# Weights converted in the first batch's first stage, stores issued by ACT, most of batch 1's first stage moved into the main loop, and the transform put ahead of the inner product

## The chip, the cores and the metric

The kernel runs on one core of a Trainium2 chip. A core has TensorE (PE, with its weight loads shown apart as PEld), VectorE (DVE), ScalarE (ACT), GpSimd (POOL), SyncE (SP, which here only issues transfers) and 16 DMA engines. The metric is the device time of one execution in microseconds; the runs before have a median of 1624.6 us (1624.46 to 1625.23, three runs).

## The reference

For 8 batches of 3136 rows by 256 columns the input is filtered in the frequency domain along the rows and then goes through a gated feed-forward layer:

```python
X = np.fft.rfft(x, axis=1)
y = np.fft.irfft(X * (filt_r + 1j * filt_i)[None], n=3136, axis=1)
h = np.maximum(y @ w_in, 0.0)                  # 256 -> 1024
conv = sum(conv_w[k] * shifted(h, k - 1) for k in range(3))   # along the rows, zero padded
out = (h / (1.0 + np.exp(-conv))) @ w_out      # 1024 -> 256
```

The weights w_in, conv_w and w_out arrive as float64.

## The kernel before, in words

**Transform.** The 3136-point transform is done by matrix products in four stages of 14 tiles each (a tile is a pair of the 28 columns of a 112 x 28 arrangement of the rows, 512 columns wide). Stage 1 multiplies rows of x by tables (line 231, `by_column`), ACT copies the bank (`store`, line 226) and a transfer (227) stores it in the DRAM buffer `a_dram` of the batch. Stage 2 (`second`, 235 and 238) reads `a_dram` back; the filter follows as three DVE passes (`filt`, 244 to 246) and a POOL addition (247). Stage 3 is `by_column` again, its result is stored in `b_dram`. Stage 4 (`fourth`, 255) reads `b_dram` and makes y. Stages 2 and 4 need all 14 tiles of the stage before them. All values are split in a high and a low part, so that three fp32r products stand for one fp32 product: y's high part is an ACT pass (145), its low part a subtraction on DVE (148) or POOL (151).

**Ahead of the main loop.** Batch 0 goes through its four stages here. In the code before, the 16 weight pieces (8 times one of w_in and one of w_out) are turned from float64 to f32 by seven DVE instructions and one POOL addition a pair (`to_f32`, 159 to 173) and split by ACT (145) and POOL (151). These steps are handed out as a generator, four at a time, among the tiles of the second and third stage, and six at a time among those of the fourth. Also among the tiles of the fourth stage stands the whole first stage of batch 1. Row tiles have 6, 5 and 4 buffers by stage, a PSUM pool has 5 banks. SP issues every transfer, in an order that a scheduler sets; PE, DVE, ACT and POOL keep the order of the code (`manual_schedule`).

**Main loop.** The 8 batches are cut in 56 units of 448 rows, and a step m is one of the 8 feature blocks of a unit: 448 steps, 56 a batch. In a step PE does `inner` (176 to 178, y times w_in, six matmuls into one of four banks), and `project` of the step six earlier (471 to 473, nine or twelve matmuls). Between, ACT does `relu` (427), `centre` (431), `sigmoid` (438) and the rounding of g (145); DVE two more taps (435) and the gate (441); POOL the low part of g (151). When a unit's projection is complete, DVE copies it out (`evacuate`, 486). The transform of batch t, its stages 2 to 4, and stage 1 of batch t+1 ride in the 56 steps of batch t-1: a table `plan` says which transform tiles a step holds. `transform(op)` does a tile's matmuls into one of two banks (`ps_t`), `from_bank(op)` empties the bank a step later: ACT copies it for stages 1 and 3, DVE filters it for stage 2 and copies it for stage 4. Inputs are loaded five tiles ahead (`tin`), and a stage's loads wait until the stage before is stored in full. Engines work in order, so an instruction that waits holds up all that stand behind it on its engine.

Of the kernel before, what the change touches and what calls it, by code (L numbers as in the profile page):

```python
# [124 lines left out]
def tile_fft_filter_gated_ffn(  # L125
# [98 lines left out]
    def store(pool, kind, b, q, ps, bufs, tag):  # L224
        st = pool.tile([112, 2, D], F32, name=tag, bufs=bufs)
        nc.scalar.activation(st, ps[0:112].rearrange("p (j d) -> p j d", d=D), AF.Copy)
        nc.sync.dma_start(out={"1": a_out, "3": b_out}[kind][b][:, pair(q)], in_=st)
# [32 lines left out]

    with (
        tc.tile_pool(name="sp", bufs=2) as sp,
        tc.tile_pool(name="sps", bufs=5, space=bass.MemoryType.PSUM) as sps,
        tc.manual_schedule(engines=COMPUTE),
# [3 lines left out]
        def load_weights(k):  # L268
            raws[k] = raw = sp.tile([128, 2, 512], I32, name="raw")
            for part, src in enumerate((w_in, w_out)):  # L270
                nc.sync.dma_start(out=raw[:, part], in_=src[:, 512 * k:512 * k + 512])

        def convert_conv():
            n = 3 * NF
            raw = sp.tile([128, 2, 512], I32, name="raw")
            nc.sync.dma_start(out=raw[:, 0, 0:2 * n], in_=conv_w)
            yield
            em = sp.tile([128, 2, 512], I32, name="em", bufs=1)
            yield from to_f32(cw.rearrange("p k f -> p (k f)"), raw[:, 0, 0:2 * n], em[:, 0, 0:n], em[:, 1, 0:n])

        def convert_weights():

            for k in range(8):
                raw = raws.pop(k)
                em = sp.tile([128, 2, 512], I32, name="em", bufs=1)
                ws = sp.tile([128, 2, 256], F32, name="ws", bufs=1)
                yield from to_f32(ws.rearrange("p t n -> p (t n)"), raw.rearrange("p t n -> p (t n)"), em[:, 0], em[:, 1])
                yield
                parts = [[t.rearrange("p a b -> p (a b)")[:, 256 * k:256 * k + 256] for t in w] for w in (wi, wo)]
                for part, (wh, wl) in enumerate(parts):  # L290
                    hi_act(wh, ws[:, part])
                yield
                for part, (wh, wl) in enumerate(parts):
                    lo_pool(wl, ws[:, part], wh)
                    yield
                if k < 6:
                    load_weights(k + 2)

        def table(kind, c):
            k, src = {"1": (112, s1), "3": (120, i1)}[kind]  # L300
            tabs[kind, c] = t = sp.tile([120, 4, 112], F32, name=f"tab{kind}", bufs=3)[0:k]
            nc.sync.dma_start(out=t, in_=src[:, 4 * c:4 * c + 4])
# [6 lines left out]
        def copy_filter(q):  # L309
# [3 lines left out]
            if q == NP - 1:  # L313
                nc.sync.dma_start(out=f[92:93, 1, 0], in_=nyq)

        def psum():
            return sps.tile([128, 512], F32, name="ps")

        csteps, wsteps = convert_conv(), convert_weights()

        def x_load(q):
            rows["1", q] = load_in(sp, "1", 0, q, 6, "x")

        def a_load(q):
            rows["2", q] = load_in(sp, "2", 0, q, 5, "a")

        for c in range(3):
            table("1", c)
            x_load(2 * c)
            x_load(2 * c + 1)  # L330
        nc.sync.dma_start(out=s2_sb, in_=s2[:, 0:120])
        nc.sync.dma_start(out=s2s_sb, in_=s2s[:, 0:120])
        nc.sync.dma_start(out=m2_sb, in_=m2)
        for q in range(NP):
            ps = psum()
            by_column(ps, tabs["1", q // 2][:, 2 * (q % 2):2 * (q % 2) + 2], rows.pop(("1", q)))
            store(sp, "1", 0, q, ps, 3, "sa")
            if q % 2 and q // 2 + 3 < 7:
                table("1", q // 2 + 3)
# [324 lines left out]
```

## Time and profile before

| what | value |
|---|---|
| median of the runs | 1624.6 us |
| profiled execution, its own time | 1620.7 us |
| its span, first to last instruction | 1618.9 us |
| PE busy, share of the span | 1527.6 us, 94% |
| DVE, ACT, POOL busy | 1203.6, 1202.6, 878.3 us |
| bytes moved, mean rate | 238.7 MB, 147 GB/s |
| first inner product of the main loop | 152 us |

The profile is one execution. Its windows give busy time of each engine in a stretch of the span, its groups give instructions by line with their mean duration, and its waits give who waited for whom; a releaser in it is inferred. Busy PE time counts overlapping matmuls once, so the time of a step is read from the starts of its first matmuls. The mean over the whole span hides that the first 152 us are worked by other engines than the rest.

### The profile page before, as it was taken

The numbers are of one execution on the slowest core, as the hardware profiler recorded it, in microseconds if no ns is written. First come the engines' busy times: TensorE is split into PE (matmuls) and PEld (weight loads), VectorE is DVE, ScalarE is ACT, GpSimd is POOL, SyncE is SP. The second block draws the span as 40 slices with busy tenths as digits, with TensorE's granted clock in tenths as the row PEclk, the third lists the DMA queues.
The fourth block names the chain that finished last, engine by engine and source line by source line (L and its number), as shares of the span: only waits on it lengthen the run. The fifth ranks groups of instructions, "written<-read, shape, count | busy, mean of one in ns | idle before, by whom it ended". The sixth has DMA issues, their size and how long they took to land.

```text
span 1618.9 us, 28466 instructions
## 1 busy us (share of the span) xinstructions
PE 1527.6 (94%) x9424; PEld 1363.0 (84%) x9424; DVE 1203.6 (74%) x1966; ACT 1202.6 (74%) x2623; POOL 878.3 (54%) x1170
## 2 busy tenths in 40 slices
PE   4658999999999999999999999999999999999999
PEld 2237788998899887998899988899889988899998
DVE  0875887768876788667877688767887788777776
ACT  3326667986688766987678866788668866799987
POOL 0541454755566555664557555575556745576554
PEclk8758999999999999999999999999999999999999
DMA  9768655355554555446553565545554435320001
GB/s 284 209 205 252 185 167 168 108 166 171 161 164 129 168 157 176 132 133 174 183 177 106 143 190 167 160 115 172 168 163 147 125 119 174 97 75 24 23 24 37
DMA packets 171491, 238.73 MB, mean 147 GB/s; under 512 B 16696, under 2 KB 119121, under 8 KB 171345
## 3 DMA queue, kind: packets, MB, share of 16 engines
q1 hardware_dynamic: 171345, 236.92, 49.3%
q8 instruction: 75, 1.23, 0.3%
q14 instruction: 71, 0.58, 0.1%
HBM read 159.78 MB, written 77.07 MB: 146 GB/s over the span
## 4 chain that ended last, share of the span: by engine, by line
PE 73%; issue 9%; DVE 6%; POOL 6%; DMA 3%; ACT 2%; SPq 1%; POOLq 0%; DVEq 0%; ACTq 0%
PE po L471 10%; PE po L472 9%; PE po L473 9%; PE ps_h L177 9%; PE ps_h L178 9%; PE ps_h L176 9%; PE ps_t L231 8%; PE ps_t L255 5%; POOL g L151 4%; PE ps_t L235 2%; DVE t L435 2%; POOL gm L151 1%; DMA a_dram<-sa 1%; DVE v L246 1%; DVE v L245 1%
## 5 line engine op out<-in xcount | busy, mean ns | idle before, releaser
L435 DVE SCALAR_TENSOR_TENSOR t<-ps_h,cw,t 128x448 f32<-128x448 f32 x896 | 609.2, 680 | 283.0 <-ACT t L431 278.3
L151 POOL TENSOR_TENSOR g<-t,g 128x384 fp32r<-128x384 f32 x448 | 455.1, 1016 | 182.5 <-ACT g L145 72.8
L431 ACT ACTIVATE t<-ps_h,cw 128x448 f32<-128x448 f32 x448 | 284.9, 636 | 231.1 <-POOL gm L151 206.2
L471 PE MATMUL po<-wo,g 128*128 128x256 f32 x1344 | 413.5, 308 | 1.9 <-DVE ot L486 1.9
L473 PE MATMUL po<-wo,g 128*128 128x256 f32 x1344 | 374.4, 279 | 0.0
L472 PE MATMUL po<-wo,g 128*128 128x256 f32 x1344 | 374.2, 278 | 0.0
L247 POOL TENSOR_TENSOR z<-z,v 120x512 f32<-120x512 f32 x112 | 147.6, 1318 | 390.0 <-DVE v L246 341.3
L176 PE MATMUL ps_h<-y,wi 128*128 128x450 f32 x896 | 330.8, 369 | 1.2 <-ACT y L145 1.2
L177 PE MATMUL ps_h<-y,wi 128*128 128x450 f32 x896 | 330.2, 369 | 0.6 <-DVE y L148 0.6
L178 PE MATMUL ps_h<-y,wi 128*128 128x450 f32 x896 | 328.3, 366 | 0.0
L441 DVE TENSOR_TENSOR t<-ps_h,t 128x448 f32<-128x448 f32 x448 | 275.7, 616 | 0.6 <-ACT t L438 0.6
L427 ACT ACTIVATE ps_h<-ps_h 128x450 f32<-128x450 f32 x448 | 250.9, 560 | 32.6 <-PE ps_h L178 30.8
L471 PEld LDWEIGHTS po<-wo,g 128*128 128x128 f32 x1344 | 253.6, 189 | 21.2 <-issue 9.9
L472 PEld LDWEIGHTS po<-wo,g 128*128 128x128 f32 x1344 | 253.5, 189 | 13.4 <-issue 10.3
L438 ACT ACTIVATE t<-t 128x448 f32<-128x448 f32 x448 | 255.9, 571 | 0.9 <-DVE t L435 0.8
L473 PEld LDWEIGHTS po<-wo,g 128*128 128x128 f32 x1344 | 253.7, 189 | 0.0
L145 ACT ACTIVATE g<-t 128x384 fp32r<-128x384 f32 x448 | 231.9, 518 | 10.4 <-PE po L472 9.7
L151 POOL TENSOR_TENSOR y<-z,y 128x448 fp32r<-128x448 f32 x98 | 139.2, 1421 | 124.0 <-ACT y L145 110.1
L178 PEld LDWEIGHTS ps_h<-y,wi 128*128 128x128 f32 x896 | 168.8, 188 | 14.2
L176 PEld LDWEIGHTS ps_h<-y,wi 128*128 128x128 f32 x896 | 169.6, 189 | 9.4 <-issue 1.6
L177 PEld LDWEIGHTS ps_h<-y,wi 128*128 128x128 f32 x896 | 169.1, 189 | 7.8 <-issue 1.1
L151 POOL TENSOR_TENSOR gm<-t,gm 128x64 fp32r<-128x64 f32 x448 | 145.9, 326 | 0.0
(73 smaller groups left out, 1992.9 us busy)
## 6 DMA issues: line engine op xcount, KB each, us to landing
filt<-in_filt SPq DMA_DIRECT2D x98, 512.0 KB, 4.2
tin<-a_dram SPq DMA_DIRECT2D x98, 224.0 KB, 3.4
b_dram<-st SPq DMA_DIRECT2D x98, 224.0 KB, 4.2
tin<-b_dram SPq DMA_DIRECT2D x98, 224.0 KB, 2.7
out<-ot SPq DMA_DIRECT2D x84, 256.0 KB, 3.1
tin<-in_x SPq DMA_DIRECT2D x84, 224.0 KB, 2.8
a_dram<-st SPq DMA_DIRECT2D x84, 224.0 KB, 3.0
tab<-in_i SPq DMA_DIRECT2D x98, 105.0 KB, 3.9
```

Of the source, the lines that this page charges most:

```text
L151: nc.gpsimd.tensor_tensor(out=dst, in0=src, in1=hi.bitcast(F32), op=ALU.subtract)
L176: nc.tensor.matmul(ps, lhsT=wh, rhs=rh, start=start, stop=False, **kw)
L177: nc.tensor.matmul(ps, lhsT=wh, rhs=rl, start=False, stop=False, **kw)
L178: nc.tensor.matmul(ps, lhsT=wl, rhs=rh, start=False, stop=stop, **kw)
L427: nc.scalar.activation(hs[u, f], hs[u, f], AF.Relu)
L431: nc.scalar.activation(t, hs[u, f][:, 1:SUB + 1], AF.Copy, scale=cw[:, 1, f:f + 1])
L435: nc.vector.scalar_tensor_tensor(out=t, in0=h[:, k:SUB + k], scalar=cw[:, k, f:f + 1], in1=t, op0=ALU.mult, op1=ALU.add)
L438: nc.scalar.activation(ts[u, f], ts[u, f], AF.Sigmoid)
L441: nc.vector.tensor_mul(ts[u, f], hs.pop((u, f))[:, 1:SUB + 1], ts[u, f])
L471: nc.tensor.matmul(o, lhsT=gh, rhs=wo[0][:, f], start=first, stop=False, skip_group_check=True)
L472: nc.tensor.matmul(o, lhsT=gh, rhs=wo[1][:, f], start=False, stop=False, skip_group_check=True)
L473: nc.tensor.matmul(o, lhsT=gl, rhs=wo[0][:, f], start=False, stop=last, skip_group_check=True)
```

## The change

Ahead of the main loop: the row tiles share one tag with 14 buffers, so that a stage's loads need not wait for buffers; the first-stage tables have 7 buffers and stay for batch 1; the PSUM pool has 8 banks. The conversion of the weights now runs among the tiles of batch 0's first stage, in whole pairs, with two buffers for its intermediates. The stores of batch 0's first and third stage, and of four tiles of batch 1's first stage, are issued by ACT in place of SP, behind the copy they store. SP also keeps the order of the code in this part. Only the first four tiles of batch 1's first stage (`AHEAD`) are done there.

In the main loop: the other ten tiles of batch 1's first stage are put in steps 0 to 6, so that its second stage starts at step 10 (4 before), its third at 13 (7), and its fourth stage has steps 44 to 53 (37 to 52). The first-stage tiles of batch 2 take other free steps. For later batches the table is as it was. In every step the transform's matmuls now come ahead of the inner product, `relu` behind the copy of the transform's bank, and `evacuate` at the start of the next step, which leaves it at the same place in DVE's order.

```diff
-    def store(pool, kind, b, q, ps, bufs, tag):
+    def store(pool, kind, b, q, ps, bufs, tag, queue=nc.sync):
...
-        nc.sync.dma_start(out={"1": a_out, "3": b_out}[kind][b][:, pair(q)], in_=st)
+        queue.dma_start(out={"1": a_out, "3": b_out}[kind][b][:, pair(q)], in_=st)
...
+    AHEAD = 4
-        tc.tile_pool(name="sps", bufs=5, space=bass.MemoryType.PSUM) as sps,
-        tc.manual_schedule(engines=COMPUTE),
+        tc.tile_pool(name="sps", bufs=8, space=bass.MemoryType.PSUM) as sps,
+        tc.manual_schedule(engines=COMPUTE | {mybir.EngineType.SP}),
...
+        def column_stage(kind, b, q, r):
+            ps = sps.tile([128, 512], F32, name="ps")
+            by_column(ps, tabs[kind, q // 2][:, 2 * (q % 2):2 * (q % 2) + 2], r)
+            store(sp, kind, b, q, ps, 3, "ss", nc.scalar)
...
+        for c in range(7):
+            table("1", c)
+            load("1", 0, 2 * c)
+            load("1", 0, 2 * c + 1)
+            if c == 0:
+                load_conv()
+            if c < 2:
+                load_weights(c)
...
+        convert_conv()
         for q in range(NP):
+            column_stage("1", 0, q, rows.pop(("1", q)))
+            if q % 2 == 1:
+                for _ in convert(q // 2):
+                    pass
+                if q // 2 + 2 < 8:
+                    load_weights(q // 2 + 2)
+            if q >= 4 and q % 2 == 0:
+                split_weights(q // 2 - 2)
+        for q in range(4):
+            load_filter(q)
+        for c in range(2):
+            table("3", c)
+        for q in range(NP):
+            load("2", 0, q)
+        split_weights(5)
+        for _ in convert(7):
+            pass
+        split_weights(6)
+        split_weights(7)
...
-            if i + 5 < NP:
-                a_load(i + 5)
-            for _ in range(4):
-                next(wsteps, None)
...
+        for q in range(AHEAD):
+            load("1", 1, q)
+        for q in range(AHEAD):
+            column_stage("1", 1, q, rows.pop(("1", q)))
         for q in range(NP):
-            ps = psum()
-            by_column(ps, tabs["1", q // 2][:, 2 * (q % 2):2 * (q % 2) + 2], rows.pop(("1", q)))
-            store(sp, "1", 1, q, ps, 3, "sa")
...
-        at2, at4 = 4, [37 + 17 * q // NP for q in range(NP)]
+        at2, at4 = (10, [44 + 10 * q // NP for q in range(NP)]) if t == 1 else (4, [37 + 17 * q // NP for q in range(NP)])
...
+        if t == 1:
+            for q in range(AHEAD, NP):
+                s = (q - AHEAD) * 7 // (NP - AHEAD)
+                used.add(s)
+                put(s, "1", 1, q)
...
-            if a := at(m):
-                inner(*a)
-            if p1:
-                relu(*p1)
+            if p7:
+                evacuate(*p7)
             for op in old:
                 from_bank(op)
             want_in()
             for op in new:
                 transform(op)
+            if a := at(m):
+                inner(*a)
             if p1:
+                relu(*p1)
                 centre(*p1)
...
             if p1:
                 tap(*p1, 2)
             if p6:
-                evacuate(*p6)
+                project(*p6)
```

How this moves the instructions is seen at three places. The first is ACT from its start, in the changed kernel: `ss` is the copy of a first-stage bank, `wi` and `wo` are high parts of converted weights (`ws`).

```order
L195 ACTIVATE cw<-cw 128x1
L226 ACTIVATE ss<-ps 112x512
L227 DMA a_dram_57<-ss 112x2x256
L226 ACTIVATE ss<-ps 112x512
L227 DMA a_dram_57<-ss 112x2x256
L226 ACTIVATE ss<-ps 112x512
L227 DMA a_dram_57<-ss 112x2x256
L226 ACTIVATE ss<-ps 112x512
L227 DMA a_dram_57<-ss 112x2x256
L226 ACTIVATE ss<-ps 112x512
L227 DMA a_dram_57<-ss 112x2x256
L145 ACTIVATE wi_82<-ws 128x256
```

Before, ACT did the 14 copies in a row here and then the copies of the filter; now each store, and from the fifth tile on each pair of weight splits, stands between two copies. The second place is PE at the start of the main loop, before (`ps_h` is the bank of an inner product, `ps_t` that of a transform):

```order
L176 MATMUL ps_h<-y_695,wi_82 128x450
L177 MATMUL ps_h<-y_696,wi_82 128x450
L178 MATMUL ps_h<-y_695,wi_83 128x450
L176 MATMUL ps_h<-y_695,wi_82 128x450
L177 MATMUL ps_h<-y_696,wi_82 128x450
L178 MATMUL ps_h<-y_695,wi_83 128x450
L231 MATMUL ps_t<-tin,tab 112x256 x2
```

and in the changed kernel, where the piece shows step 2, with two transforms, and the transform of step 3:

```order
L231 MATMUL ps_t<-tin,tab 112x256 x4
L176 MATMUL ps_h<-y_741,wi_82 128x450
L177 MATMUL ps_h<-y_742,wi_82 128x450
L178 MATMUL ps_h<-y_741,wi_83 128x450
L176 MATMUL ps_h<-y_741,wi_82 128x450
L177 MATMUL ps_h<-y_742,wi_82 128x450
L178 MATMUL ps_h<-y_741,wi_83 128x450
L231 MATMUL ps_t<-tin,tab 112x256 x2
```

The transform has moved ahead of the inner product, and three of these first seven steps hold two of them. The third place is PE in step 49 of the changed kernel, where the fourth stage of batch 1 and the first stage of batch 2 meet (`po` is the projection's bank):

```order
L457 MATMUL po_2792<-wo_84,g_2722 128x256
L458 MATMUL po_2792<-wo_85,g_2722 128x256
L459 MATMUL po_2792<-wo_84,g_2723 128x256
L255 MATMUL ps_t<-m_sb,tin 128x112 x8
L231 MATMUL ps_t<-tin,tab 112x256 x2
L176 MATMUL ps_h<-y_741,wi_82 128x450
```

Before, no step had more than two transforms; here three (twice four matmuls of stage 4 and two of stage 1) stand in one step, ahead of its inner product, and there are two banks.

More of the change, by code (lines that the diff above doesn't have):

```diff
@@ L275, in convert_conv @@
[L275 to L297, printed above, removed]
+            n, raw = 3 * NF, raws.pop("c")
@@ new lines, in convert_conv, with convert, split_weights @@
+            em = sp.tile([128, 2, 512], I32, name="em")
+            for _ in to_f32(cw.rearrange("p k f -> p (k f)"), raw[:, 0, 0:2 * n], em[:, 0, 0:n], em[:, 1, 0:n]):
+                pass
+        def convert(k):
+            raw = raws.pop(k)
+            em = sp.tile([128, 2, 512], I32, name="em")
+            ws[k] = w = sp.tile([128, 2, 256], F32, name="ws")
+            yield from to_f32(w.rearrange("p t n -> p (t n)"), raw.rearrange("p t n -> p (t n)"), em[:, 0], em[:, 1])
+        def split_weights(k):
+            w = ws.pop(k)
+            parts = [[t.rearrange("p a b -> p (a b)")[:, 256 * k:256 * k + 256] for t in h] for h in (wi, wo)]
+            for part, (wh, wl) in enumerate(parts):
+                hi_act(wh, w[:, part])
+            for part, (wh, wl) in enumerate(parts):
+                lo_pool(wl, w[:, part], wh)
@@ L350, in tile_fft_filter_gated_ffn @@
+        for q in range(4):
[6 more added lines that the diff above has]
+        for _ in convert(7):
+            pass
+        split_weights(6)
+        split_weights(7)
+        table("3", 2)
         for q in range(4):
             copy_filter(q)
-        for q in range(5):
-            a_load(q)
         pss = {}
@@ L371, in tile_fft_filter_gated_ffn @@
                 copy_filter(i + 2)
[L372 to L390 removed]
+        for q in range(AHEAD):
+            load("1", 1, q)
+        for q in range(AHEAD):
+            column_stage("1", 1, q, rows.pop(("1", q)))
+        for q in range(NP):
+            load("4", 0, q)
+        for q in range(NP):
+            ps = sps.tile([128, 512], F32, name="ps")
             fourth(ps, rows.pop(("4", q)))
@@ L394, in tile_fft_filter_gated_ffn @@
             lo_dve(yl, as_y(ps[:, 0:4 * N1]), yh)
-            if q + 4 < NP:
-                rows["4", q + 4] = load_in(sp, "4", 0, q + 4, 4, "br")
-            for _ in range(6):
-                next(wsteps, None)
-        for _ in wsteps:
-            pass
     yps.append(ctx.enter_context(tc.tile_pool(name="y_odd", bufs=1, reuse_waits="tile")))
@@ L503, in tile_fft_filter_gated_ffn @@
             put(w + at4[q], "4", t, q)
+        if t == 1:
[3 more added lines that the diff above has]
+                put(s, "1", 1, q)
         free = [s for s in range(53) if s not in used]
-        free = sorted(free + [s for s in range(0, 53) if s // NF % 2 == 0 and s not in free][::-1][:NP - len(free)])
+        free = sorted(free + [s for s in range(at2, 53) if s // NF % 2 == 0 and s not in free][::-1][:NP - len(free)])
         if t + 1 < B:
```

72 lines of the change are left out of this document (18 added, 54 removed).

## The prediction

> **What bounds it now.** I read the stages first, as windows whose edges are the places where the work changes: the first stage of batch 0 (0 to 43 us), its second and third stages with the weights converted among them (to 109), its fourth stage with batch 1's first stage among it (to 152), then the main loop, 56 steps a batch.
>
> ```profile
> 0.00:43.00 43.00, 17.30 (x57) 11.56 (x58) 3.05 (x11) 14.88 (x24) 1.52 (x8) 0.82 0.94 283
> 43.00:109.00 66.00, 43.68 (x90) 21.64 (x90) 59.25 (x82) 23.40 (x46) 36.79 (x31) 0.68 0.66 196
> 109.00:152.00 43.00, 29.33 (x164) 25.41 (x164) 20.30 (x27) 22.49 (x34) 7.53 (x12) 0.80 0.85 253
> 152.00:342.00 190.00, 182.85 (x1113) 162.21 (x1114) 141.94 (x233) 142.47 (x314) 104.11 (x137) 0.99 0.55 162
> 342.00:530.00 188.00, 185.72 (x1173) 167.89 (x1173) 144.21 (x238) 146.46 (x323) 108.30 (x145) 1.00 0.53 158
> ...
> 20.00:30.00 10.00, 4.74 (x16) 2.84 (x16) 0.00 (x0) 2.49 (x5) 0.00 (x0) 0.88 1.07 336
> ```
>
> The columns are the window, its length, busy time on PE, weight loads, DVE, ACT and POOL, then clock, DMA share and GB/s. Four different limits stand here. To 43 us the DMA engines are 94% busy at 283 GB/s. To 109 us DVE is busy 59 of 66 us. To 152 us the DMA engines are back at 85%. From there PE is busy 183 of 190 us and 186 of 188. So before 152 us a byte or a DVE instruction is worth something and PE time nothing; after it the reverse.
>
> The main loop starts with the first inner product, and a transform in it has a plain price on PE. The third and fourth rows below are a step without a transform, the first, second and last one with one (a step is from one of these starts to the next; all have the same nine projection matmuls).
>
> ```profile
> L176 PE MATMUL ps_h<-y,wi x896: 362/367/938, 152.1 to 1604.7; 128*128 128x450 f32 x180
> ...
> 401.22 0.37 PE L176 MATMUL ps_h<-y,wi 128*128 128x450 f32 x1
> 402.45 1.02 PE L235 MATMUL ps_t<-tin,s_sb 112*120 112x512 f32 x2
> 404.37 0.37 PE L176 MATMUL ps_h<-y,wi 128*128 128x450 f32 x1
> ...
> 1590.26 0.37 PE L176 MATMUL ps_h<-y,wi 128*128 128x450 f32 x1
> 1592.51 0.37 PE L176 MATMUL ps_h<-y,wi 128*128 128x450 f32 x1
> ```
>
> 404.37 - 401.22 = 3.15 us with a transform, 1592.51 - 1590.26 = 2.25 us without: 0.90 us for a transform of 512 columns. The inner product takes 402.45 - 401.22 = 1.23 us.
>
> **Part 1, ahead of the main loop: -30 us.** What moves there is bytes and DVE work.
>
> ```profile
> DMA packets 27533, 35.99 MB, mean 237 GB/s; under 512 B 3226, under 2 KB 18739, under 8 KB 27526
> ...
> x<-in_x SPq DMA_DIRECT2D x28, 224.0 KB, 4.5
> a_dram<-sa SPq DMA_DIRECT2D x28, 224.0 KB, 4.1
> f<-in_filt SPq DMA_DIRECT2D x28, 128.0 KB, 3.2
> tab<-in_s SPq DMA_DIRECT2D x14, 196.0 KB, 4.3
> raw<-in_w_in SPq DMA_DIRECT2D x8, 256.0 KB, 3.9
> tab<-in_i SPq DMA_DIRECT2D x7, 210.0 KB, 4.6
> filt<-in_filt SPq DMA_DIRECT2D x2, 512.0 KB, 5.8
> tab<-in_s SPq DMA_DIRECT2D x4, 98.0 KB, 3.1
> ```
>
> These are the DMA issues up to 152 us: count, size, median time to landing. In the changed order SP issues, ahead of the first load of the second stage: 14 row tiles of 224 KB, 7 tables of 196, all 16 weight pieces of 256, 8 filter pieces of 128, 2 tables of 210, five inputs of the main loop (224), three small tables (98), one filter of 512 and about 180 KB of constants; ACT issues the 14 stores of 224. Sum 15,290 KB = 15.7 MB, at the 283 GB/s of the first stage 55 us. So the second stage starts later than now: 55 against 43. The conversions, which now lie in it, run under this: eight of them, from a first weight piece that lands in some 8 us. They are off the path as long as they end before the loads do; the rows of DVE in the second stage say what one takes.
>
> ```profile
> L246 DVE SCALAR_TENSOR_TENSOR v<-ps,f 56x512 f32<-56x512 f32 x14 | 9.7, 693 | 0.4
> L244 DVE TENSOR_TENSOR z<-ps,f 120x512 f32<-120x512 f32 x14 | 9.7, 692 | 10.3 <-PE ps L235 9.9
> L245 DVE TENSOR_TENSOR v<-ps,f 56x512 f32<-56x512 f32 x14 | 9.6, 684 | 0.4
> L226 ACT ACTIVATE sb<-ps 112x512 f32<-112x512 f32 x14 | 8.1, 579 | 7.5 <-issue 7.5
> L163 DVE TENSOR_TENSOR em<-em 128x512 int32<-128x512 int32 x5 | 6.2, 1232 | 0.2
> L311 ACT ACTIVATE f<-f 56x512 f32<-56x512 f32 x10 | 6.3, 630 | 27.1 <-DMA f<-in_filt 25.1 <-DVE v L246 1.8
> ```
>
> Of DVE's 59.25 us the filter is 9.7 + 9.7 + 9.6 = 29.0, so 30 us are conversions, of which this stage holds five to six (the row of em, one instruction of each, counts 5): about 5.4 us each. Eight end near 8 + 8 x 5.4 = 51 us. That is close under 55: where they run over, every microsecond shows, since the filter copies stand behind them on ACT.
>
> The second and third stages then need on DVE 29 us, on ACT 14 x (2 x 0.63 + 0.58) = 26 us, and on the DMA engines the 14 loads and 14 stores of 224 KB, 20 filter pieces, 5 tables of 210, four row tiles of batch 1, a filter and a table: 11,390 KB = 11.7 MB, 41 us at 283 GB/s. The DMA engines are the longest, so the last copy for a store is on ACT at 55 + 41 = 96 us, where it now stands at 109:
>
> ```profile
> 108.95 0.58 ACT L226 ACTIVATE sb<-ps 112x512 f32<-112x512 f32 x1
> 109.56 0.33 SPq L227 DMA_DIRECT2D b_dram<-sb  x1
> ...
> 114.40 1.82 SPq L221 DMA_DIRECT2D br<-b_dram  x4
> ...
> 117.70 2.02 PE L255 MATMUL ps<-m_sb,br 112*128 112x112 f32 x8 [10.01 <-DMA br<-b_dram]
> ...
> L148 DVE TENSOR_TENSOR y<-ps,y x14: 968/991/1014, 120.8 to 151.9; 128x448 fp32r<-128x448 f32 x14
> ```
>
> From that copy to the first fourth-stage matmul is 117.70 - 108.95 = 8.8 us (store, landing, load), which stays. Behind it 14 tiles now take 34 us, since batch 1's loads and stores share the DMA engines; with ten of those tiles gone the pair of passes over y is left, one on ACT, one on DVE, 0.99 us each and overlapped: 1.0 + 14 x 0.99 + 0.99 = 15.9 us. The loop starts at 96 + 8.8 + 15.9 = 121 us; with about a microsecond for the four batch 1 tiles that ACT copies ahead I take **122**, 30 earlier than 152.
>
> The unseen price is ACT as the issuer of 32 stores. No row has it; from below it is nothing (SP is relieved of the same), from above it is that a waiting store or split on ACT blocks the copies behind it and the DMA engines run no better than their present mean, 237 GB/s: 27.3 MB / 237 = 115, and 115 + 25.7 = 141 us. The best row, 336 GB/s, gives 81 + 25.7 = 107. I stay with 283, the row with the same mix of loads and stores issued without a DVE bound; the ends are -45 and -11 us.
>
> The Trainium skill (DMA: Bandwidth & Descriptors, Issuing engines are not separate DMA queues) says that transfers issued by different engines run on the same 16 DMA engines, and that a second issuer saves only sequencer time. By it the ACT queue adds no rate and 122 stands; were it a second path, 107 would be nearer. No row here has an ACT store, so the trace cannot say.
>
> **Part 2, the main loop: +19 us.** Ten of the 14 first-stage tiles of batch 1 become transforms in steps 0 to 6: 10 x 0.90 = **+9 us** of PE, with nothing to hide it, as PE is the bound there. Their copies, 10 x 0.58 = 5.8 us, come on ACT in seven steps that have little else on PE; half of it shows, **+3** (0 to 6). Batch 1's second stage must wait until the last of those stores has landed; the order leaves three steps (some 9 us) against the 8.8 us of the chain above, and 14 fourth-stage tiles of batch 1 now share ten steps with five of batch 2, two of which hold three transforms for two PSUM banks. PE waits there for DVE's copy. The nearest waits are these:
>
> ```profile
> PE po L471 <- DVE ot L486: 15.7, 17, 1.3
> PE ps_t L235 <- PE ps_h L178: 7.0, 12, 0.7
> PE ps_t L238 <- PE ps_h L178: 2.3, 4, 0.6
> ```
>
> The longest of them, 1.3 us, twice, and as much again for the late load: **+4** (0 to 9).
>
> The transform ahead of the inner product costs no instruction, but moves a wait. A bank is free when DVE has read it:
>
> ```profile
> 195.20 0.37 PE L176 MATMUL ps_h<-y,wi 128*128 128x450 f32 x1
> 196.36 0.69 DVE L246 SCALAR_TENSOR_TENSOR v<-ps_t,filt 56x512 f32<-56x512 f32 x1
> 197.15 1.09 PE L235 MATMUL ps_t<-tin,s_sb 112*120 112x512 f32 x2 [0.56 <-PE ps_h L178]
> ...
> 203.45 0.69 DVE L246 SCALAR_TENSOR_TENSOR v<-ps_t,filt 56x512 f32<-56x512 f32 x1
> ```
>
> The filter ended at 197.05, and the transform that takes its bank began at 197.15 (the row's releaser is not it). The inner product from 195.20 on had covered 1.23 us of that wait; put behind the transform, it covers none, and DVE gets its input 0.90 us later. On the other hand the filters come every 203.45 - 196.36 = 7.09 us per two steps here, set by DVE, POOL and ACT among themselves, so PE is slaved to them in this phase whatever its own order: what it waits longer at the transform it waits shorter at the next projection (the 15.7 us row), which now stands 1.23 us later after the transform. What is lost is the lead at the end of a phase, at most 1.23 + 0.90 = 2.1 us in each of seven batches, 15 us; what can be won is the 15.7. I take 0.4 a batch, **+3**.
>
> **Sum.** -30 + 9 + 3 + 4 + 3 = -11 us. The profiled execution took 1620.7 us (span 1618.9); 1609.7 after. The median of the runs is 3.9 us above it, which I keep: 1624.6 - 11 = **1613.6**, say 1614.
>
> **Rivals.** (a) *The loads run at the best rate and the projections lose their wait*: the loop starts at 107 (-45), and +9 +3 +4 with half of the 15.7 us back: 1624.6 - 45 + 16 - 8 = 1588. For it: 336 GB/s in the trace, and all loads of the first stage need no buffer first. Against: that row has few stores. (b) *ACT blocks*: the loop starts at 141, net 1624.6 - 11 + 19 + 0 = 1633. For it: ACT's present waits on a filter load, 25.1 us, would stand ahead of stores. Against: ACT is busy only 23 of 66 us there. (c) *The other side: the uncovered bank wait*. Place: the second-stage transforms of the main loop, 14 a batch. If DVE does not come earlier to the same extent, two thirds of them, some 65 in seven batches, wait half of the 1.23 us: +40, and 1614 - 3 + 40 = 1651. It turns the change into a loss from 14 us on, that is from 0.2 us a transform. Against: the 7.09 us rhythm, which allows no such sum over a phase. (d) *The moved stage comes back*: ten loads, ten stores and ten tables are 5.6 MB, 20 us at 283 GB/s, in steps that take 7 x 1.23 + 10 x 0.90 = 18 us; with the landing after it the second stage waits 8 us more, and the sum is 1622: hardly a change.
>
> **Chances.** The forecast 0.5, (a) 0.2, (b) 0.1, (c) 0.1, (d) 0.1. A measurement of this kernel tells about 0.2% from no change, 3.2 us here: faster is under 1621.4, slower over 1627.8. Faster: nearly all of the forecast, (a), a third of (d): 0.73. Same: 0.08. Slower: (b), (c) and the forecast's tail: 0.19. The range reaches from close above (a) to (b): 1593 to 1633; the forecast's own is 1603 to 1625.
>
> **What would show it.** The first inner product near 122 us (107 and 141 are the other cases); the first load of the second stage landing near 55, the last copy for a stage-3 store on ACT near 96; then 14 passes over y at 1.0 us. DVE in the second stage about 29 us of 41, not 59 of 66. Batch 1's 56 steps at 206 us, the later ones at 188 to 192 as now. In PE's waits less on the evacuation (15.7) and more on transforms. A loop start later than 133 us, or more than 4 us added to each later batch, makes the forecast wrong.

## The result

The changed kernel takes 1600.5 us (median of four runs, 1598.1 to 1602.8) against 1624.5 for the kernel before, a ratio of 0.9862 (95% interval 0.9838 to 0.9886). It is 24 us faster, where 11 were forecast. The profiled execution took 1598.1 us (span 1596.3, 22.6 below the span before), so the traces have nearly all of the difference to account for.

### The profile after

The windows of the changed kernel, cut again where the work changes: batch 0's first stage with the conversions (to 59 us), the second and third stage (to 104), four tiles of batch 1 and the fourth stage (to 124), the main loop. Columns as before: PE, PEld, DVE, ACT and POOL busy, clock, DMA share, GB/s.

```profile
0.00:59.00 59.00, 18.81 (x56) 11.90 (x56) 37.28 (x59) 14.41 (x30) 20.79 (x26) 0.71 0.91 277
59.00:104.00 45.00, 31.58 (x88) 16.94 (x89) 32.29 (x47) 25.20 (x45) 23.20 (x25) 0.88 0.81 240
104.00:124.00 20.00, 17.84 (x128) 16.14 (x127) 10.69 (x12) 14.48 (x18) 0.00 (x0) 0.93 0.77 219
124.00:320.00 196.00, 190.93 (x1157) 170.04 (x1157) 142.45 (x235) 149.04 (x325) 103.21 (x136) 1.00 0.62 178
320.00:508.00 188.00, 186.10 (x1172) 168.35 (x1171) 144.00 (x239) 146.72 (x324) 109.31 (x146) 1.00 0.54 158
...
20.00:30.00 10.00, 7.33 (x24) 4.89 (x24) 0.00 (x0) 1.48 (x4) 0.00 (x0) 0.83 1.04 341
30.00:40.00 10.00, 0.00 (x0) 0.00 (x0) 9.52 (x16) 1.80 (x4) 3.50 (x4) 0.58 0.96 285
...
50.00:60.00 10.00, 0.93 (x1) 0.47 (x2) 9.66 (x13) 1.45 (x4) 6.34 (x6) 0.50 0.87 248
```

The loop's batches take what they took: 188 us for the second. DVE's work has moved into the first stage, but not evenly: from 20 to 30 us it does nothing while the DMA engines run at 341 GB/s, and from 30 to 60 it is 96% busy.

One row gives the loop apart from what lies ahead of it, the starts of the first and the last inner product:

```profile
L176 PE MATMUL ps_h<-y,wi x896: 362/375/776, 125.6 to 1582.1; 128*128 128x450 f32 x180
```

The loop begins with its first PE instruction, here a transform at 124.04; before it was the inner product at 152.1. So the loop **starts 28.0 us earlier** (152.05 - 124.04), and from there to its last inner product it takes 1582.1 - 124.0 = 1458.1 us instead of 1604.7 - 152.1 = 1452.6: **5.5 us longer**. Forecast were 30 earlier and 19 longer. (By the sign that the prediction names, the first inner product, the start is 125.6 us, 26.5 earlier, and the loop counted from there is 3.9 us longer.) The loop is where the forecast missed; ahead of it the sum was right, but several of its terms were not, as the experiments show.

How the 124 us come about stands in single rows of the timeline (start, duration, engine, line, operation, and in brackets idle time of the engine with its releaser):

```profile
54.65 5.40 SPq L221 DMA_DIRECT2D rows<-a_dram  x10
...
59.07 3.59 PE L235 MATMUL ps<-rows,s_sb 112*120 112x512 f32 x4 [30.93 <-ACT wo L145]
...
65.41 0.69 DVE L244 TENSOR_TENSOR z<-ps,f 120x512 f32<-120x512 f32 x1 [2.85 <-ACT f L311]
...
103.78 0.60 ACT L226 ACTIVATE ss<-ps 112x512 f32<-112x512 f32 x1 [3.28 <-PE ps L231]
...
110.26 2.01 PE L255 MATMUL ps<-m_sb,rows 112*128 112x112 f32 x16 [1.51 <-DMA rows<-b_dram]
...
124.04 1.89 PE L231 MATMUL ps_t<-tin,tab 112*112 112x256 f32 x8
```

The second stage's loads are issued from 54.65 us on, its first matmul is at 59.07, but the first filter only at 65.41: it waits for ACT's copy of a filter (L311), which stands behind the weight splits on ACT. The waits of DVE up to 104 us (engine, tile and line, what it waited for: us in total, times, longest) name the ends of the conversion chain, and one in the filter:

```profile
DVE em L159 <- DMA raw<-in_w_out: 14.2, 2, 13.8
...
DVE z L244 <- DMA f<-in_nyq: 4.6, 1, 4.6
DVE z L244 <- ACT f L311: 2.9, 1, 2.9
```

One wait of 13.8 us for raw weights is the idle slice from 20 to 30: the third weight pair is loaded behind all row tiles. The one-row load `in_nyq`, which the change also moves from SP to ACT, makes DVE wait 4.6 us; in the kernel before no such wait is listed.

### The profile page after: what moved, and what is told of

It reads as the page before. It is cut to its first block, busy times and chain, and to the rows that moved or that the text cites. A ratio compares the mean times of both kernels' runs of the same rounds, so it can differ in the third digit from the quotient of the medians.

```text
span 1596.3 us, 28479 instructions
## 1 busy us (share of the span) xinstructions
PE 1517.3 (95%) x9424; PEld 1360.7 (85%) x9424; DVE 1197.7 (75%) x1966; ACT 1201.8 (75%) x2623; POOL 875.6 (55%) x1170
## 4 chain that ended last, share of the span: by engine, by line
PE 67%; issue 12%; POOL 8%; DVE 7%; DMA 3%; ACT 2%; SPq 0%; POOLq 0%; ACTq 0%; DVEq 0%
PE po L457 9%; PE po L458 9%; PE po L459 9%; PE ps_h L176 9%; PE ps_h L177 8%; PE ps_h L178 8%; PE ps_t L231 7%; POOL g L151 5%; PE ps_t L255 5%; DVE t L421 2%; PE ps_t L235 2%; POOL gm L151 2%; DMA a_dram<-ss 1%; POOL z L247 1%; PE ps L231 1%
## 5 line engine op out<-in xcount | busy, mean ns | idle before, releaser
L176 PE MATMUL ps_h<-y,wi 128*128 128x450 f32 x896 | 410.2, 458 | 0.0
L457 PE MATMUL po<-wo,g 128*128 128x256 f32 x1344 | 374.3, 279 | 0.4
L458 PE MATMUL po<-wo,g 128*128 128x256 f32 x1344 | 374.0, 278 | 0.0
L459 PE MATMUL po<-wo,g 128*128 128x256 f32 x1344 | 373.5, 278 | 0.0
L247 POOL TENSOR_TENSOR z<-z,v 120x512 f32<-120x512 f32 x112 | 143.3, 1280 | 355.2 <-DVE v L246 308.6
L177 PE MATMUL ps_h<-y,wi 128*128 128x450 f32 x896 | 328.9, 367 | 0.4 <-DVE y L148 0.4
L178 PE MATMUL ps_h<-y,wi 128*128 128x450 f32 x896 | 328.6, 367 | 0.0
L413 ACT ACTIVATE ps_h<-ps_h 128x450 f32<-128x450 f32 x448 | 243.7, 544 | 67.8 <-PE ps_h L178 66.7
L151 POOL TENSOR_TENSOR y<-z,y 128x448 fp32r<-128x448 f32 x98 | 138.2, 1413 | 121.7 <-ACT y L145 119.1
L176 PEld LDWEIGHTS ps_h<-y,wi 128*128 128x128 f32 x896 | 169.5, 189 | 37.4 <-issue 22.3
L177 PEld LDWEIGHTS ps_h<-y,wi 128*128 128x128 f32 x896 | 170.2, 190 | 35.0 <-issue 22.6
```

What stands on the lines that cost most here:

```text
L151: nc.gpsimd.tensor_tensor(out=dst, in0=src, in1=hi.bitcast(F32), op=ALU.subtract)
L176: nc.tensor.matmul(ps, lhsT=wh, rhs=rh, start=start, stop=False, **kw)
L177: nc.tensor.matmul(ps, lhsT=wh, rhs=rl, start=False, stop=False, **kw)
L178: nc.tensor.matmul(ps, lhsT=wl, rhs=rh, start=False, stop=stop, **kw)
L413: nc.scalar.activation(hs[u, f], hs[u, f], AF.Relu)
L457: nc.tensor.matmul(o, lhsT=gh, rhs=wo[0][:, f], start=first, stop=False, skip_group_check=True)
```

## The experiments

All of them compute the whole reference. "Loop starts" is its first PE instruction in the trace, "loop takes" the time from there to the start of the last inner product, which is read from the L176 row of each kernel.

| kernel | median us | ratio to before, 95% interval | loop starts | loop takes |
|---|---|---|---|---|
| before | 1624.5 | | 152.1 | 1452.6 |
| the change | 1600.5 | 0.9862 (0.9838 to 0.9886) | 124.0 | 1458.1 |
| 1 change, old order in a step | 1602.6 | 0.9866 (0.9845 to 0.9887) | 127.9 | 1459.1 |
| 2 before, new order in a step | 1618.6 | 0.9970 (0.9958 to 0.9982) | 151.2 | 1451.5 |
| 3 change, first stage of batch 1 back | 1615.5 | 0.9950 (0.9931 to 0.9968) | 146.3 | 1453.2 |
| 4 as 3, late second stage kept | 1609.6 | 0.9918 (0.9902 to 0.9933) | 145.9 | 1449.2 |
| 5 change, stores issued by SP | 1610.8 | 0.9916 (0.9891 to 0.9941) | 136.9 | 1458.2 |
| 6 change, conversions late | 1615.8 | 0.9949 (0.9929 to 0.9969) | 138.5 | 1461.5 |
| 7 change, last filter loaded whole | 1600.0 | 0.9849 (0.9828 to 0.9869) | 123.5 | 1458.7 |
| 8 as 7, weights loaded earlier | 1597.6 | 0.9834 (0.9815 to 0.9854) | 125.8 | 1457.5 |
| 9 as 8, five store buffers | 1598.4 | 0.9848 (0.9831 to 0.9864) | 126.7 | 1458.0 |
| 10 change, five store buffers | 1600.1 | 0.9862 (0.9845 to 0.9878) | 125.5 | 1458.4 |
| 11 as 8, loop's first loads earlier | 1596.8 | 0.9835 (0.9819 to 0.9852) | 121.5 | 1458.0 |
| 12 as 11, five store buffers | 1597.0 | 0.9837 (0.9820 to 0.9853) | 121.7 | 1459.0 |

The loop takes 1457.5 to 1459.1 in all kernels with ten moved tiles but one (6, whose first transform runs ahead of a fourth stage that isn't done), whatever lies before it. So the two columns can be judged apart. The change and kernels 5 and 7 to 12 have the same loop and differ by up to 1.5 us in it, so a smaller difference of two loops is not told apart from chance. The start is less sure still: kernel 1 and the change have the same code ahead of the loop, and their first inner products are at 127.9 and 125.6 us. Each kernel has one trace, of one run: that of kernel 8 took 1599.3 us where its median is 1597.6, that of kernel 11 took 1595.5 where its median is 1596.8.

### 1 and 2: the order inside a step

Kernel 1 is the change with the old order in a step; kernel 2 is the old kernel with the new order alone, by the same lines the other way round.

```diff
-            if p7:
-                evacuate(*p7)
+            if a := at(m):
+                inner(*a)
+            if p1:
+                relu(*p1)
             for op in old:
                 from_bank(op)
...
-            if a := at(m):
-                inner(*a)
...
-                project(*p6)
+                evacuate(*p6)
```

> The changed kernel with the old order inside a step (inner product ahead of the transform, relu ahead of the copy of the bank, evacuation in its old place). Theory S (the waits of the first 56 steps went because the second stage now starts at step 10, with the backlog of the first steps worked off): 1598 to 1603 us, the first 56 steps 194 to 197 us. Rival T (they went because the transform now stands first): 1606 to 1611 us, with 5 to 9 us more in the first 56 steps. The step of the prediction that priced the order at 3 us over seven batches: 1597 us, the saving in the later batches.

> The kernel before with only the new order inside a step. Theory S: 1622 to 1626 us, no change, and the waits of steps 6 to 14 stay (some 5 us). Rival T: 1613 to 1618 us, these waits gone. By the prediction 3 us slower than before, 1627 us.

The loop takes 1 us less with the new order in both pairs (1458.1 against 1459.1, 1451.5 against 1452.6), no more than chance can make; the traces put it at the loop's first steps. With the inner product first, PE waits behind its first matmul for the last part of y (0.72 us in kernel 1, 0.57 in the kernel before) and soon runs at half its clock (0.50 from 130 to 132 us in kernel 1, from 154 to 157 in the kernel before). With the transform first, which needs no y, the clock there is 1.00 in kernel 2 and in the change (not in kernels 3 and 4, below). Kernel 1's first 56 steps take 196.6 us, as theory S had it. The medians of kernel 2 and of the kernel before go further apart (5 us, with 1623.6 for the kernel before in that job; 1618.6 lies between the ranges of the two theories), which the trace of one execution doesn't show; 1 us is what is explained. The waits of PE over the whole run, in the changed kernel:

```profile
PE ps_t L235 <- PE po L459: 12.8, 26, 0.6
...
PE ps_t L238 <- PE po L459: 1.8, 3, 0.6
...
PE ps_t L231 <- PE po L459: 0.8, 3, 0.3
```

Before, the evacuation cost 15.7 us (the row in the prediction) and the transforms 7.0 and 2.3. The evacuation is gone from the list, the transforms wait 12.8, 1.8 and 0.8, each time 0.6 us at most. That is the exchange the prediction described. It wins almost nothing: in the six batches behind the first the shown waits of PE fall from 18.5 to 13.4 us, and the time of those batches by 0.7. A wait that goes from this list is no gain by itself where PE follows the rhythm of other engines.

### 3 and 4: the moved first stage, and the late start of the second

Kernel 3 does batch 1's whole first stage ahead of the loop again, with the old steps for batch 1. Kernel 4 does the same but keeps the second stage's start at step 10.

```diff
-    AHEAD = 4
+    AHEAD = NP
...
-        at2, at4 = (10, [44 + 10 * q // NP for q in range(NP)]) if t == 1 else (4, [37 + 17 * q // NP for q in range(NP)])
+        at2, at4 = (4, [37 + 17 * q // NP for q in range(NP)])
```

(The last pair of lines is in kernel 3 alone.)

> The changed kernel with all 14 first-stage tiles of batch 1 ahead of the main loop and the old places of batch 1's other stages (second stage from step 4). Both theories: the loop starts 10 to 18 us later than the 124 us of the changed kernel, since ten loads and stores of 224 KB come back there (4.6 MB, 16 us at 283 GB/s), and ten transforms of 0.9 us leave the loop. Theory S: the first 56 steps take 188 to 191 us, with the waits of before in steps 6 to 14; 1605 to 1613 us in all. Rival T: 180 to 184 us, 1598 to 1604 us.

> As the run before it, but with batch 1's second stage from step 10 on and its fourth stage in steps 44 to 53, as in the changed kernel. Theory S: the waits of steps 6 to 14 go, the first 56 steps take 181 to 186 us, 4 to 8 us less than with the start at step 4. Rival T: no less than with the start at step 4, rather 2 to 3 us more for the crowded steps 44 to 53.

This pair splits the loop's 5.5 us. From kernel 3 to kernel 4 only the start of the second stage and the steps of the fourth move: 1453.2 to 1449.2, **-4.0**, and the medians fall by 5.8. From kernel 4 to the change only ten tiles move (and the places of batch 2's first-stage tiles with them): the loop takes **+8.9** (1458.1 - 1449.2; ten transforms at 0.90 are 9.0) and starts 145.9 - 124.0 = 21.9 earlier. That is more than the 18 that the prediction's third figure implied (34 us of fourth stage cut to 15.9), and puts kernel 3 above the ranges expected for it.

That 8.9 stands so near 9.0 is partly luck. Kernels 3 and 4 begin their loop at half clock: before it PE has been idle for 5.59 and 5.82 us, by the profile until DVE's last pass over y. The windows of the first two steps, kernel 3 and then kernel 2, which has the same steps in the same order (the clock is the third number from the end):

```profile
146.25:150.35 4.10, 4.09 (x10) 3.37 (x11) 0.00 (x0) 0.60 (x1) 0.00 (x0) 0.50 0.25 64
150.35:152.94 2.59, 2.59 (x11) 2.18 (x10) 1.08 (x2) 1.76 (x3) 0.00 (x0) 0.81 0.49 129
...
151.15:154.10 2.95, 2.42 (x11) 1.85 (x11) 1.00 (x1) 1.26 (x2) 0.00 (x0) 1.00 0.84 247
154.10:156.20 2.10, 2.10 (x11) 1.84 (x10) 0.62 (x1) 1.66 (x3) 0.00 (x0) 1.00 0.60 200
```

Two steps take 6.69 us against 5.05, and these 1.6 us are nearly all of the 1.7 by which kernel 3's loop is longer than kernel 2's; from the third inner product on the two loops differ by 0.1 us. Kernel 4's first two steps take 6.78 us, at the same clock, while the change begins at 1.00. So an estimate for the ten tiles by themselves is 8.9 + 1.7 = 10.6 us, the 9.0 of their matmuls and 1.6 more.

The waits of PE in batch 1's window show what the late start removes. In kernel 3 (the window from the loop's start to the next batch):

```profile
PE ps_t L235 <- ACT st L226: 3.2, 4, 1.3
PE ps_t L235 <- PE po L459: 2.2, 4, 0.7
PE ps_t L238 <- PE po L459: 0.6, 1, 0.6
```

and in kernel 4, over the same stretch:

```profile
PE ps_t L231 <- DVE v L246: 1.2, 1, 1.2
PE po L457 <- DVE ot L472: 1.1, 1, 1.1
PE ps_t L235 <- PE po L459: 0.6, 1, 0.6
```

With 0.7 us of shorter ones that is 6.0 us against 3.6, 2.4 of the 4.0. What goes are the 3.2 us in which second-stage transforms of the early start wait for ACT's copies; by the eleventh inner product kernel 4 is 3.2 us ahead of kernel 3 (28.3 us after its start against 31.5), so most of the gain does lie there. Why ACT is late was not tried further. In the kernel before, the same stretch (152 to 342 us) holds

```profile
PE ps_t L235 <- PE ps_h L178: 3.0, 5, 0.7
PE po L471 <- DVE ot L486: 2.9, 3, 1.3
```

and 2.4 us of shorter ones, 8.3 in all; in the change (124 to 320 us) the five rows add to 5.0, of which the longest are

```profile
PE ps_t L235 <- PE po L459: 2.0, 4, 0.6
PE ps_t L231 <- DVE z L567: 1.2, 2, 0.6
PE ps_t L231 <- DMA tab<-in_s: 0.9, 1, 0.9
```

### 5: the stores back on SP

```diff
-            store(sp, kind, b, q, ps, 3, "ss", nc.scalar)
+            store(sp, kind, b, q, ps, 3, "ss", nc.sync)
```

> The changed kernel with the stores ahead of the main loop issued by SP again, in the place that the code gives them. Theory Q (a store of its own queue matters because SP holds loads that wait in front of it): the loop starts 4 to 12 us later, 1604 to 1612 us. Rival B (both queues feed the same 16 engines and ACT is idle enough either way): within 2 us of the changed kernel.

The loop starts 12.8 us later (136.9), the median is 10.3 us higher. The filter starts 1 us earlier and ends 4 later than in the change; most of the loss lies behind it. SP's longest wait in this kernel, up to 124 us,

```profile
SPq L227 <- ACT ss L226: 27.1, 17, 4.2
```

its issues behind the third stage,

```profile
108.39 1.85 SPq L221 DMA_DIRECT2D rows<-in_x  x4
114.50 4.16 SPq L227 DMA_DIRECT2D a_dram<-ss  x4
118.70 7.66 SPq L221 DMA_DIRECT2D rows<-b_dram  x13
```

and those of the changed kernel:

```profile
89.61 5.88 SPq L221 DMA_DIRECT2D rows<-in_x  x4
106.79 9.59 SPq L221 DMA_DIRECT2D rows<-b_dram  x14
```

On SP in order, each store waits for its copy and everything behind it waits too: batch 1's four row loads come at 108 instead of 90, their tiles and stores at 114, and only behind those the fourth stage's loads, 118.7 instead of 106.8. ACT pays 0.31 us an issue for it, and has the idle time:

```profile
104.41 0.31 ACTq L227 DMA_DIRECT2D b_dram<-ss  x1
```

The rule of the Trainium skill that the prediction cited (DMA: Bandwidth & Descriptors, Issuing engines are not separate DMA queues) holds as to the rate: over the first 120 us the changed kernel moves 260 GB/s, this one 235, and both are below the 283 of the first stage before, where SP issued all. That only sequencer time is saved, usually little, does not hold here: the time of the sequencer that waits is worth 10 us. In both kernels SP keeps the order of the code; in the kernel before a scheduler set it, and the stores on SP in such an order were not tried with the rest of the change.

### 6: the conversions back among the second and third stage

```diff
-            if q % 2 == 1:
-                for _ in convert(q // 2):
-                    pass
...
             if 4 <= i + 2 < NP:
                 copy_filter(i + 2)
+            for _ in range(4):
+                next(wsteps, None)
```

> The changed kernel with the weights converted among the later stages, four and six instructions at a time, as before. Theory C (the conversions, 5.7 us of DVE each, are what holds the second stage back to 65 us, and they cost as much wherever they stand): the filter starts near 50 us, the second and third stage take about 60 us again, the loop starts between 124 and 130 us; total 1600 to 1607 us. Rival D (among the first stage they are hidden under its loads, as the prediction had it): the filter starts at 55 us or later, and the loop starts 12 us or more later than 124; 1612 us or more.

(Behind the last lines, six instructions at a time are handed out among the fourth stage, as in the kernel before.) The loop starts 14.5 us later, the median is 15.3 higher. The second and third stage begin at 41.6 us instead of 65.4, but take until 110:

```profile
41.60:110.00 68.40, 41.14 (x80) 19.29 (x78) 65.83 (x83) 22.68 (x44) 37.23 (x30) 0.62 0.74 218
```

DVE is busy 65.8 of 68.4 us here. Early conversions are worth 15 us, so theory C, by which they cost as much anywhere, fell; the loop's start is as D had it, the filter's (41.6, and not 55 or later) is not. They are hidden under the loads only in part, where the prediction had them hidden: in the changed kernel DVE's last conversion ends at 62.6 us, and the filter starts 6 us behind the second stage's first matmul. What the early place gains is that the DVE time is spent where less else needs DVE.

A part of the conversion's price is its neighbour. Two conversions follow each other in the changed kernel, the first with POOL idle (DVE, then POOL in the same microseconds):

```profile
30.34 0.42 DVE L161 TENSOR_SCALAR em<-raw 128x512 int32<-128x512 int32 x1
...
34.19 1.49 DVE L161 TENSOR_SCALAR em<-raw 128x512 int32<-128x512 int32 x1
...
34.08 1.31 POOL L173 TENSOR_TENSOR ws<-ws,em 128x512 f32<-128x512 f32 x1 [15.15 <-DVE em L171]
```

The same instruction takes 0.42 us alone and 1.49 us beside POOL's addition, ending 0.3 us after it. A conversion is 3.9 us alone (30.00 to 33.85) and 5.7 beside POOL's work for the one before it. That is what the Trainium skill (SBUF — State Buffer, SBUF: two separate sides) describes as a port pair that DVE and GpSimd lock against each other for a whole instruction; these rows agree with it, no run here takes POOL away.

### 7 to 12: where the rest of the prologue is bound

Kernel 7 loads the last filter whole, against the 4.6 us wait for the small transfer into it, 8 also loads the third weight pair with the first row tiles, against the 13.8 us wait.

```diff
+            if q == NP - 1:
+                nc.sync.dma_start(out=f, in_=filt_in[0:120, pair(q)])
+                return
...
-            if c < 2:
+            if c < 3:
                 load_weights(c)
...
-                if q // 2 + 2 < 8:
-                    load_weights(q // 2 + 2)
+                if q // 2 + 3 < 8:
+                    load_weights(q // 2 + 3)
```

> The changed kernel with the last pair's filter loaded whole from the table that the main loop uses, in place of two halves, two ACT copies and a one-row transfer that DVE is seen to wait 4.6 us for. If that wait is on the path to the loop's start, as the order of the third stage says: 3 to 5 us earlier, 1595 to 1598 us. If the stores behind it set the pace: within 1 us of the changed kernel.

> As the run before it, and a third weight pair loaded with the first rows (a fourth buffer for raw weights), so that DVE does not stand idle from 16 to 30 us. If the chain of conversions sets the start of the second stage, as theory C says, one conversion of 5.7 us is drawn forward and the filter starts 4 to 6 us earlier: 1590 to 1594 us. If the transfers set it, the earlier weights push the rows back: no gain over the run before it.

Kernel 7 starts its loop at 123.5. It does not say whether the 4.6 us were on the path, since the last filter now waits nearly as long for its own load:

```profile
DVE z L244 <- DMA f<-in_filt: 3.7, 1, 3.7
```

In kernel 8 the 13.8 us wait for weights falls to 9.2, the filter starts 4 us earlier (61.5) and the last filter, which waits for no load there, 7 us earlier (91.05 against 98.08); yet its traced loop starts at 125.8. Its median is 2.4 us below that of kernel 7 in the same job, with intervals that overlap, and 1597.6 is above the 1590 to 1594 expected of it. In kernel 8 the copies of the last third-stage tiles wait for their buffers, up to 3.48 us, until the stores of earlier ones have landed. So 9 gives the stores of 8 five buffers instead of three, and 10 those of the change:

```diff
-            store(sp, kind, b, q, ps, 3, "ss", nc.scalar)
+            store(sp, kind, b, q, ps, 5, "ss", nc.scalar)
```

> The kernel with early weights and a whole last filter, and five instead of three buffers for the copies that the prologue stores (the tables of stages 1 and 3 share seven buffers to make room). In the run before it the copies of the last third-stage tiles waited for earlier stores to land (3.48, 2.14, 1.58, 1.32 us each, on ACT), the last copy stood at 101.7 instead of some 95, and the tile loads behind it came at 104.8. Theory B (the three buffers hold back the gain): the last third-stage copy at 95 to 98, first transform of the main loop at 119 to 122, time 1591 to 1595. Theory D (the stores themselves need the DMA engines that long, buffers or not): copies come earlier but the fourth stage's first tile is loaded at 103 to 105 as before, first transform 124 to 126, time 1596 to 1600.

> The changed kernel with five instead of three buffers for the stored copies and nothing else. There the last third-stage copy waits for PE (the last filter's chain), not for a buffer, so both theories expect the third stage to end where it did (last copy 102 to 104, first transform 122 to 125, time 1597 to 1603); only if the copies of the first stage had waited for buffers too would the filter start before 63 us and the time fall by more than 3 us.

The buffers gave nothing (126.7, 125.5). The stores themselves had become slow. The DMA issues from 85 to 112 us (count, KB each, median us from issue to landing) and the total there, in the changed kernel:

```profile
DMA packets 4476, 6.17 MB, mean 228 GB/s; under 512 B 455, under 2 KB 2841, under 8 KB 4475
...
b_dram<-ss ACTq DMA_DIRECT2D x9, 224.0 KB, 2.5
```

and in kernel 9:

```profile
DMA packets 5181, 7.90 MB, mean 292 GB/s; under 512 B 543, under 2 KB 2901, under 8 KB 5180
...
b_dram<-ss ACTq DMA_DIRECT2D x8, 224.0 KB, 5.7
```

The bytes that came in are seen among SP's issues, kernel 9 first, then the change:

```profile
90.55 4.15 SPq L221 DMA_DIRECT2D tin<-in_x  x3
```

```profile
28.34 1.40 SPq L221 DMA_DIRECT2D tin<-in_x  x3
```

These are row tiles for the main loop, and its tables and filters follow them. In the change SP issues them between 28 and 42 us, between the loads of weights that wait for a buffer; with the weights loaded early they come between 84 and 100, among the stores. Kernel 11 puts them by hand behind the second stage's loads, and 12 adds the five buffers.

```diff
         for q in range(NP):
             load("2", 0, q)
+        want_in()
+        for n in range(3):
+            want_table(n)
+        want_filter(0)
```

> The kernel with early weights and a whole last filter, and the first loads of the main loop (five row tiles, three tables, one filter, some 1.9 MB) issued by SP right behind the loads of the second stage, about 60 us, where the DMA engines stood at 28% (62 to 70 us), instead of at 80 to 97 us, among the stores of the third stage. Theory B (the gain of early weights was lost because these loads took the DMA engines from the stores, whose landing rose from 2.5 to 5.7 us): the last third-stage copy at 95 to 98, the fourth stage's first tile loaded by 101 to 103, first transform of the main loop at 117 to 121, time 1590 to 1595. Theory D (the stores need that long whatever else is in flight, or the filter loads are late instead): first transform at 124 to 127, time 1596 to 1600.

> The same with five instead of three buffers for the stored copies (stages 1 and 3 share seven table buffers). With five buffers alone the first transform was not earlier (126.7 against 125.8). By theory B it now follows the run with three buffers within 2 us (117 to 121, time 1589 to 1595), since the wait for buffers was a sign of slow stores and not a cause; were the buffers a limit of their own, it would be 3 us or more earlier than that run. By theory D 124 to 127 and 1596 to 1600, as the run with three.

```profile
56.56 3.26 SPq L221 DMA_DIRECT2D tin<-in_x  x5
...
94.37 0.69 DVE L244 TENSOR_TENSOR z<-ps,f 120x512 f32<-120x512 f32 x1 [3.45 <-DMA f<-in_filt]
...
100.07 0.60 ACT L226 ACTIVATE ss<-ps 112x512 f32<-112x512 f32 x1 [0.76 <-PE ps L231]
...
121.45 1.89 PE L231 MATMUL ps_t<-tin,tab 112*112 112x256 f32 x8
```

These are rows of kernel 11. The loop starts at 121.5 (121.7 with five buffers), 4.3 us earlier than in the trace of kernel 8: better than theory D, short of most of B's bounds. The times do not follow: 1596.8 and 1597.0 us lie in theory D's range, and kernel 8 has 1597.6 (ratios to the kernel before of 0.9835, 0.9837 and 0.9834), so a part of the 4.3 us is the difference of single runs. The landing of the stores fell to 3.6 us and their buffers are no limit of their own, as B had it; the last third-stage copy is at 100.07, not 95 to 98, as the last filter waits again, 3.45 us, for its load, which lands among the stores with a 512 KB filter for the loop. Had the 7 us gained at the last filter come through, kernel 8 would have started its loop at 117 and not at 125.8. Of these 9 us 4.3 came back by the traces and about 1 by the medians. So that these loads slow the stores is shown, that this is what cost kernel 8 its gain is not; what holds the rest no run separates. Kernel 11 has the lowest median, 1596.8 us; its interval overlaps that of the change, so that it is faster is likely but not shown.

## Why the prediction was right and wrong

- **The loop, +19, was wrong; it is +5.5.** This is the step that failed, part 2's sum, and in it above all the **+4** for bank waits and late loads, which measured **-4.0**, and the **+3** for the order. The +4 added waits to a window as if those it already held would stay. They did not: the second stage, which the change starts at step 10 instead of 4, no longer meets ACT's copies at the start of the loop (kernels 3 and 4). That move stands in the description of the change; the prediction priced only what follows it. The order in a step measured -1.0 and -1.1 in the loops of the traces (and -5 in the medians of kernel 2's job) where +3 stood, inside its bounds of -15 to +15; the -1 is no more than chance can make, and stands with the clock of the loop's first steps. The **+9** for ten transforms and the **+3** for their copies come nearest: the moved tiles cost 8.9, or some 10.6 if kernel 4's start at half clock is taken out. So 10.6 - 4.0 - 1.1 = 5.5. (The 0.90 us behind the +9 stand, though the prediction counts its rows wrongly: the step without a transform is the one from 1590.26 to 1592.51.)
- **The loop's start, -30, was right at -28.0, by errors that cancel, which is luck.** The second stage's loads were due at 55 and are issued at 54.65. That the conversions end under them, near 51, was wrong: DVE stood 13.8 us without weights, a conversion beside POOL's work took 5.7 us and not 5.4, the last one ended at 62.6, and the filter starts at 65.4. The 41 us set by the DMA engines were 38 (65.4 to 103.8), paced by DVE (14 filters at 2.16 us) and held up by the last filter's 4.6 us wait. So the last copy stood at 103.8, not 96: 8 us late. From there the chain is 6.5 us (103.78 to 110.26) where 8.8 were kept, and the fourth stage is 13.8 us to the loop's start where 15.9 and 1 for the copied tiles were counted, as the first transform doesn't wait for the last pass over y (which ends at 126.4). The 14 passes take the predicted 1.0 us apiece.
- **The price of an ACT store** was left between -15 and +19 us of loop start and taken as nothing. One issue is 0.31 us, and the whole is worth -10 us against SP in the order of the code (kernel 5), inside the -30. Rival (b) put ACT in the role of the engine that blocks; the engine that blocks is SP. What the 14 row buffers and the eight PSUM banks are worth by themselves no run separates.
- **Rival (c)**, the uncovered bank wait, did not come: the six later batches are 0.7 us shorter in all, and transforms in them wait 0.6 us at most. This agrees with the argument of the 7.09 us rhythm. **Rival (d)** did not come either: no step of the first window shows a wait on a load over 0.9 us. **Rival (a)** named the right side with the wrong mechanism: the first stage did not run at 336 GB/s throughout (277 in the mean), and the projections' wait went without giving time back.

## What to carry to other kernels

When a change shifts a stage in a schedule, take off the waits that stand in its old place before adding those of the new one, and price both from the waits of that window. When two loops are compared by their length, look first whether they start at the same clock: half a clock in the first two steps was 1.6 us here, as much as the differences in question. Put transfers that wait for an engine's result on a queue whose later transfers depend on it anyway; on the common queue, kept in the order of the code, each of them delayed every load behind it here. And when a wait on a prologue's path is removed and the end does not move, look at what else was issued into the time that was freed: the transfers that had filled an idle slot go somewhere, and may land on the next stage's stores.

## What was not expected of the hardware

An integer pass of DVE over 128 x 512 elements takes 0.42 us alone and 1.49 us beside POOL's addition, though the two share no data; the chain of conversions goes from 3.9 to 5.7 us a pair beside it. A store of 224 KB lands 2.5 us after its issue when 6.17 MB move in 27 us, and 5.7 us when 7.90 MB do: its latency more than doubles at 28% more traffic, with 3.6 us at 6.59 MB (kernel 7) and at 7.14 MB (kernel 11) between.

A third thing is the clock of PE at the start of the fourth stage. In kernel 9 PE does nothing from 105 to 110 us, and runs at half its clock in the next 5:

```profile
105.00:110.00 5.00, 0.00 (x0) 0.00 (x0) 0.00 (x0) 1.19 (x2) 0.00 (x0) 0.99 0.79 256
110.00:115.00 5.00, 3.22 (x15) 3.25 (x16) 0.14 (x1) 0.99 (x1) 0.00 (x0) 0.50 1.08 288
```

There, the first passes over y are 1.7 us apart (ACT at 113.84, 115.54) and later 1.0. In the changed kernel four tiles of batch 1 keep PE busy up to the fourth stage, and the window from 104 to 124 has a clock of 0.93. Half a clock behind idle time is also seen at the start of the loop in kernels 3 and 4: 5.6 and 5.8 us without a matmul, then a first step of 4.1 us at a clock of 0.50.
